# Small pads between the operand buffers of a float32r feed-forward stage

## The chip, the cores and the metric

The kernel runs on one core of one Trainium2 chip. The metric is the device time of one execution in microseconds (us), as the median over runs.

## The reference

One layer with 2048 rows of 640 channels. A modulation row (`c`, `w_mod`) gives scales and shifts. A state-space convolution over the rows comes first, then a gated feed-forward network (FFN) with an inner width of 1728:

```python
h = _layernorm(x, axis=-1) * (1 + ca) + sa
x = x + ga * _A_ref(h, A_log_A_real, A_A_imag, A_C_real, A_C_imag, A_log_dt, A_D_skip)
h = _layernorm(x, axis=-1) * (1 + cb) + sb
x = x + gb * _B_ref(h, B_w1, B_w3, B_w2)
...
    def _B_ref(x, w1, w3, w2):
        gate = jnp.einsum("bsd,df->bsf", x, w1)
        up = jnp.einsum("bsd,df->bsf", x, w3)
        h = _silu(gate) * up
        out = jnp.einsum("bsf,fd->bsd", h, w2)
        return out
```

`_A_ref` builds a convolution kernel for each channel and applies it with FFTs. All arrays are float32.

## The kernel before

**Stages.** About the first 390 us belong to the convolution: tables and kernels for five blocks of 128 channels, and Fourier products as matmuls in plain float32. Then come some tens of microseconds in which the first pieces of the FFN are made ready (`tail_tasks`, with `gates` at line 1302), and from about 440 us to the end the FFN (`ffn`, line 1412). The order of the work up to the FFN is a planner's (`Plan.place`, by ranks and durations); in the FFN it is the order of the code.

**The FFN's products.** Each float32 operand is split into a high and a low part in the type float32r (`split`: ScalarE rounds, VectorE takes the difference), and a product is three matmuls: high weights by high rows, high weights by low rows, low weights by high rows (`three`, line 852). Every one has a 128x128 weight tile and streams 512 columns of a "moving" operand. The 2048 rows are four blocks of 512, taken two at a time. `groups` (line 1422) goes over the tiles of 128 inner channels; for two blocks at once it saves one product in eight by sums and differences of operands (`factors`, `x_sums`), so that a tile takes 54 matmuls into gate and up values (`X`, `c` in the profile) and 15 into the output sums (`acc`, `down`, line 1032). `late` (line 1454) then does the second block's output sums and transposes.

**Buffers.** A tile is asked of a pool by its tag; tags get addresses in the order in which they are first asked for. Each address below is in bytes within a partition. Two pools matter here.
- `wp`, on the left side of the memory: the split weights `wh0`, `wl0` ... `wh7`, `wl7` (1024 bytes each, made by `pair`, line 816), the raw weights `wr`, the split output weights `w2` (three buffers) and their raw form `w2r`. All of these sizes are multiples of 512, and the pool begins at 35744, so every weight tile that a matmul reads begins at residue 416 modulo 512.
- `fp`, on the right side: among others the moving operands `x0h`, `x0l` ... `x8h`, `x8l` (`x_new`, line 739) and `ah`, `al` (lines 883 and 1342). These sizes are multiples of 512 too, and every moving operand begins at residue 480 modulo 512 (`x0h` at 136160, `ah` at 183264 and 185312).

The pool `const` already holds a tile named `pad` of 128 bytes that nothing reads or writes (line 311): `cols` before it ends at 1788, rounded to 1792, and `sc` after it begins at 1920.

Of the kernel before, what the change touches and what calls it, by code (L numbers as in the profile page):

```python
# [10 lines left out]
F32 = mybir.dt.float32  # L11
F32R = mybir.dt.float32r
# [6 lines left out]
P = 128  # L19
# [9 lines left out]

EXPS = ((0, 0, 0, 64.0), (0, 1, 0, 1.0), (1, 0, 0, 512.0), (1, 1, 4, 8.0), (1, 2, 0, 8.0))  # L30
LOADS = 20
G0 = 17
SIGN = -2 ** 31
RANKS = """
# [113 lines left out]
class InOrder:  # L148

    def __init__(self, k, eng):  # L150
        self.k, self.eng, self.prev = k, eng, None
# [130 lines left out]
class K:  # L282
    def __init__(self, tc, ctx, io):
        self.tc, self.nc, self.ctx = tc, tc.nc, ctx
        for k, v in io.items():
            setattr(self, k, v)

# [449 lines left out]
        return (t[:, k % 2 if n == 2 else 0] for t in X[g])  # L737

    def x_new(self, tag, name, n):
        return [self.fp.tile([P, n, 512], F32R, name=f"{tag}{x}{name}", tag=tag + x) for x in "hl"]  # L740

    TS = (("T1", "x2"), ("T2", "x3"), ("T3", "x4"), ("T4", "x6"))

# [70 lines left out]
        return t[:, 0], t[:, 1]  # L814

    def pair(self, i, name):
        return tuple(self.wp.tile([P, 2, P], F32R, name=f"w{x}{i}_{name}", tag=f"w{x}{i}") for x in "hl")

    def operand(self, i, name, v, eng):

# [62 lines left out]
    def hidden_split(self, b, m, a, eng):  # L883

        A = self.nc.scalar
        ah, al = (self.fp.tile([P, 512], F32R, name=f"a{x}{b}_{m}", tag=f"a{x}", bufs=2) for x in "hl")
        if m < 13:
            self.split(ah, al, a, eng)
            return ah, al
        th = self.tmp(f"t{b}_{m}")  # L890
        A.activation(ah[:64], a[64:], AF.Copy)
        A.activation(th[64:], ah[:64].bitcast(F32), AF.Copy)
        self.nc.vector.tensor_sub(ah[64:], a[64:], th[64:])
        return ah, None
# [169 lines left out]
    def paced(self, dst, src):  # L1064

        ins = self.nc.sync.dma_start(dst, src)
        n = len(self.pace)
        if 1 < n < LOADS:
            self.tc.add_manual_dep(ins.ins, self.pace[-2 if n < 6 else -4].ins.name,
# [3 lines left out]
    def tail_tasks(self, border, cut):  # L1073
# [10 lines left out]
        def add(name, eng, took, f, after=(), rank=0.0, **kw):  # L1084
            plan.add(name, eng, took, f, after, rank, own=True, **kw)
# [3 lines left out]
        def load(name, src, dst, size, after=(), pool="change", **kw):  # L1089
            i = n_load[0]  # L1090
            n_load[0] += 1
            loads.append(name)
            early = i < LOADS
            add(name, "SP", 0, lambda: self.paced(dst(), src), [pool, *after] + (loads[max(i - 2, 0):i][:1] if early else ["izb0"]), -60 + .1 * i,
# [180 lines left out]
        def plain(b, tiles, p, rank, after):  # L1275
# [23 lines left out]
            for r, m in enumerate(tiles):  # L1299
                gates(b, m, banks, f"{b}.{m}", last, names, (rank if b or m == 1 else G0) + .5 + .1 * r)  # L1300

        def gates(b, m, banks, n, last, names, r):
            t = {}

            def alloc(x):
                return self.h_tile(m) if b else self.tmp(f"a{b}{m}")

            def th():
                t[0] = self.tmp(f"th{n}")
                if m < 13:  # L1310
                    return A.activation(t[0], banks[m][0], AF.Tanh, scale=0.5)
                t[1] = alloc(m)
                A.activation(t[0][64:], banks[m][0][:64], AF.Tanh, scale=0.5)
                A.activation(t[1][64:], banks[m][0][:64], AF.Copy)

            def st():
                if m < 13:
                    t[1] = alloc(m)
                    V.scalar_tensor_tensor(t[1], t[0], 1.0, banks[m][0], op0=ALU.add, op1=ALU.mult)
                else:  # L1320
                    V.scalar_tensor_tensor(t[1][64:], t[0][64:], 1.0, t[1][64:], op0=ALU.add, op1=ALU.mult)

            def mu():
                if m < 13:
                    V.tensor_mul(t[1], t[1], banks[m][1])
                else:
                    V.tensor_mul(t[1][64:], t[1][64:], banks[m][0][64:])
                if b:
                    self.h[m] = t[1]
            one = [("tmp", 1)]  # L1330
            two = [("tmp", 1, "*")] if b == 0 else []
            room = ["T1l.0", "T1l.1", "T2l.0"] if b and m == 1 else []
            add("gt" + n, "ACT", .6 if m < 13 else 1.2, th, last + (room if m == 13 else []), r, take=one + (two if m == 13 else []))
            add("gs" + n, "DVE", .69, st, ["gt" + n] + (room if m < 13 else []), r, take=two if m < 13 else [],
                give=[("tmp", "gt" + n)] + (names[m, 0] if m < 13 else []))
            add("gm" + n, "DVE", .69, mu, ["gs" + n], r, give=names[m, n_of(m) - 1])
            if b:
                return
            key = [("tmp", ("gs" if m < 13 else "gt") + n + "*")]
            if m < 13:  # L1340
                def hi():
                    t[4], t[5] = (self.fp.tile([P, 512], F32R, name=f"a{x}0_{m}", tag=f"a{x}", bufs=2) for x in "hl")
                    self.high(t[4], t[1])
                add("gh" + n, "ACT", .6, hi, ["gm" + n] + (["dn0.0"] if m == 1 else []), r + .2)
                add("gl" + n, "DVE", .69, lambda: self.low(t[4], t[5], t[1]), ["gh" + n], r + .2, give=key)
            else:
                add("gl" + n, "DVE", 1.9, lambda: t.__setitem__(6, self.hidden_split(0, 13, t[1], V)), ["gm" + n], r + .3, take=[("tmp", 1)], give=key)
                add("gx" + n, None, 0, None, ["gl" + n], give=[("tmp", "gl" + n)])

            def down():  # L1350
                if m == 0:
                    self.acc = self.accumulators(0)
                self.down(self.acc, m, (t[4], t[5]) if m < 13 else t[6], (w2[m][:, 0], w2[m][:, 1]), m == 0, False)
            add("dn" + n, "PE", 3.42 if m < 13 else 2.28, down, ["gl" + n, f"w2l{m}"] + {0: [f"v1.{k}" for k in range(KT)] + ["pp1.4"], 13: ["dn0.0", "pq0.4"], 1: ["dn0.13"]}[m], r + 1, give=[("w2", f"w2h{m}")])
# [13 lines left out]
        f = {}  # L1368
# [807 lines left out]
```

## Time and profile before

| what | value |
|---|---|
| median of 3 runs | 973.41 us (972.67 to 974.1) |
| the profiled execution's own time | 972.31 us |
| span of the profiled execution | 970.5 us |
| mean granted TensorE clock | 0.975 |
| TensorE matmuls busy | 859.9 us, 89% |
| weight loads busy | 681.8 us, 70% |
| VectorE busy | 702.0 us, 72% |
| ScalarE busy | 546.4 us, 56% |
| GpSimd busy | 340.5 us, 35% |
| DMA | 127.31 MB, mean 131 GB/s |

PE stands for TensorE's matmuls, PEld for its weight loads, DVE for VectorE, ACT for ScalarE, POOL for GpSimd. The duration of a matmul in the profile holds a fixed latency besides the time in which its columns stream, so matmuls overlap; the step from one start to the next is what a row of them costs.

### The profile page before, as it was taken

Reading aid. Unit: us, or ns where it says so; the run is one execution under the profiler, and the core shown is the slowest. Engines: PE = TensorE matmul, PEld = TensorE weight load, DVE = VectorE, ACT = ScalarE, POOL = GpSimd, SP = SyncE. Lnnn points to the kernel's source line nnn. Section 1 sums busy time; section 2 is a strip of 40 time slices with the busy share of each in tenths; the row PEclk is TensorE's granted clock in tenths of the full one; section 3 lists DMA queues with packets and bytes.
Section 4 is the critical chain, followed back from the end, with each engine's and each line's share of the span. In section 5 each row is a group of like instructions: output and inputs, shape, how many; then the busy total and the mean of one; then the engine's idle time right before and its main releaser. Section 6 shows DMA issues by size and latency. Waiting matters only on the chain.

```text
span 970.5 us, 20551 instructions
## 1 busy us (share of the span) xinstructions
PE 859.9 (89%) x7985; PEld 681.8 (70%) x7985; DVE 702.0 (72%) x1395; ACT 546.4 (56%) x1022; POOL 340.5 (35%) x371
## 2 busy tenths in 40 slices
PE   1464787889899997899999999999999999999997
PEld 1132665767778884677777778888788888888775
DVE  7998899999999968886767677557456464645422
ACT  6877788979888851564434455346444344443412
POOL 1797889879799600002111111000011212120000
PEclk9996999999999999799999999999999999999999
DMA  9955453723425268935434422276342322220374
GB/s 218 275 168 191 111 136 95 177 66 106 111 80 152 74 159 206 241 118 182 122 120 139 122 96 68 82 209 194 112 134 64 102 77 86 82 82 28 108 220 133
DMA packets 110506, 127.31 MB, mean 131 GB/s; under 512 B 10568, under 2 KB 90696, under 8 KB 109128
## 3 DMA queue, kind: packets, MB, share of 16 engines
q1 hardware_dynamic: 109032, 125.21, 45.3%
q8 instruction: 63, 1.03, 0.5%
q10 hardware_dynamic: 1376, 0.79, 0.3%
q14 instruction: 35, 0.29, 0.1%
HBM read 95.82 MB, written 30.15 MB: 130 GB/s over the span
## 4 chain that ended last, share of the span: by engine, by line
PE 70%; DVE 17%; ACT 5%; issue 4%; DMA 3%; POOL 1%; SPq 1%; ACTq 0%; DVEq 0%
PE c L157 19%; PE acc L157 18%; PE X L157 12%; PE ps L157 4%; PE gu L157 3%; DVE yy L157 3%; PE kps L157 3%; PE fz L157 2%; PE fk L157 2%; DVE fp L157 2%; PE fh L157 2%; DVE hn L157 2%; DVE xx L157 2%; DVE xb L157 1%; ACT tr L157 1%
## 5 line engine op out<-in xcount | busy, mean ns | idle before, releaser
L157 PE MATMUL acc<-ah,w 128*128 128x512 f32 x560 | 173.2, 395 | 2.4 <-DMA w<-w2d 1.7
L157 PEld LDWEIGHTS acc<-ah,w 128*128 128x128 f32 x560 | 103.7, 188 | 26.4 <-issue 2.1
L157 PE MATMUL acc<-al,w 128*128 128x512 f32 x260 | 102.4, 394 | 0.0
L665 DVE TENSOR_TENSOR wl<-s,wh 128x256 fp32r<-128x256 f32 x92 | 38.9, 423 | 67.5 <-ACT wh L664 67.1
L841 POOL TENSOR_TENSOR s<-wr 128x256 f32<-128x256 f32 x22 | 16.4, 744 | 187.8 <-DMA wr<-in_w 94.8
L157 POOL TENSOR_TENSOR ph<-p,p 128x1024 int32<-128x1024 int32 x40 | 79.2, 1979 | 8.2 <-ACT tr L157 8.0
L664 ACT ACTIVATE wh<-s 128x256 fp32r<-128x256 f32 x92 | 37.6, 410 | 78.5 <-PE X L157 58.1
L157 PE MATMUL kps<-yy,xx 128*32 128x64 f32 x2560 | 51.8, 234 | 28.6 <-DVE xx L157 21.4
L157 DVE TENSOR_TENSOR yy<-yy,tr 128x512 f32<-128x512 f32 (+1 forms) x80 | 75.3, 943 | 1.2 <-ACT tr L157 0.6
L157 PEld LDWEIGHTS kps<-yy,xx 128*32 128x32 f32 x2560 | 45.1, 116 | 38.3 <-issue 22.0
L664 ACT ACTIVATE wh<-wr 128x256 fp32r<-128x256 f32 x92 | 38.4, 418 | 56.0 <-PE X L157 42.3
L842 POOL TENSOR_TENSOR s<-s,wr 128x256 f32<-128x256 f32 x22 | 16.6, 755 | 134.0 <-issue 133.9
L902 ACT ACTIVATE t<-g 128x512 f32<-128x512 f32 x44 | 27.8, 632 | 52.7 <-DVE g L866 52.7
L157 ACT ACTIVATE tr<-ph,hpi 128x512 f32<-128x512 f32 x80 | 54.6, 690 | 4.4 <-DVE xx L157 2.7
L157 PEld LDWEIGHTS acc<-al,w 128*128 128x128 f32 x260 | 48.9, 188 | 10.8 <-DVE al L665 0.3
L871 DVE SCALAR_TENSOR_TENSOR g<-t,g 128x512 f32<-128x512 f32 x48 | 33.7, 702 | 31.3 <-ACT t L902 29.3
L157 POOL TENSOR_TENSOR yy<-e,e 128x512 f32<-128x512 f32 x48 | 52.4, 1109 | 8.8 <-PE kps L157 5.9
L157 DVE TENSOR_TENSOR xx<-tr,xx 128x512 f32<-128x512 f32 x80 | 54.3, 680 | 1.1 <-ACT tr L157 1.1
L157 PE MATMUL ps<-wk,ks 128*64 128x128 f32 x640 | 42.4, 285 | 13.6 <-DVE ks L157 8.9
L157 ACT ACTIVATE tr<-ph 128x512 f32<-128x512 int32 x80 | 47.3, 598 | 12.4 <-DVE yy L157 6.5
L157 PE MATMUL ps<-wk,xb 128*64 128x128 f32 x640 | 46.1, 295 | 6.3 <-ACT sp L157 3.0
L157 PEld LDWEIGHTS ps<-wk,ks 128*64 128x64 f32 x640 | 37.0, 143 | 20.3 <-ACT hn L157 6.6
(448 smaller groups left out, 2379.7 us busy)
## 6 DMA issues: line engine op xcount, KB each, us to landing
w<-w2d SPq DMA_DIRECT2D x42, 640.0 KB, 3.9
wr<-in_w SPq DMA_DIRECT2D x50, 320.0 KB, 3.9
zd<-zt SPq DMA_DIRECT2D x40, 256.0 KB, 2.9
w2d<-w SPq DMA_DIRECT2D x14, 640.0 KB, 3.5
xs<-in_x SPq DMA_DIRECT2D x16, 320.0 KB, 11.3
hs<-hb SPq DMA_DIRECT2D x20, 256.0 KB, 2.5
xb<-hs SPq DMA_DIRECT2D x20, 256.0 KB, 4.9
iz<-zd SPq DMA_DIRECT2D x32, 160.0 KB, 5.0
```

Of the source, the lines that this page charges most:

```text
L157: self.prev = self.k.order(f(*a, **kw), self.prev)
L664: self.nc.scalar.activation(H, v, AF.Copy)
L665: eng.tensor_tensor(Lo, v, H.bitcast(F32), op=ALU.subtract)
L841: eng.tensor_tensor(s[0], u[:, 0:2], u[:, 2:4], op=ALU.add)
L842: eng.tensor_tensor(s[1], s[0], g[:, 0:2], op=ALU.subtract)
L871: V.scalar_tensor_tensor(g, th, 1.0, g, op0=ALU.add, op1=ALU.mult)
L902: tanh = lambda o, i: A.activation(o, i, AF.Tanh, scale=0.5)
```

## The change

A dictionary `PAD` gives, by tag, a number of units of 32 bytes. When one of these tags is first asked for, a small tile that nothing uses is taken from the same pool just ahead of it (`apart`), and all later buffers of the pool move up. In `fp` the entry `end` brings the sum to 512 bytes, so that what lies ahead of the first pad and behind the last keeps its residue.

```diff
+PAD = {'wh1': 1, 'wl1': 1, 'wh4': 1, 'wh3': 1, 'wl3': 1, 'wh7': 2, 'wh2': 2, 'wl2': 2, 'wl5': 1, 'wh6': 1, 'wl6': 2, 'x0l': 1, 'x4h': 2, 'x5h': 2, 'x2h': 2, 'x3h': 2, 'end': 7}
...
+        self.placed = set()
...
     def x_new(self, tag, name, n):
-        return [self.fp.tile([P, n, 512], F32R, name=f"{tag}{x}{name}", tag=tag + x) for x in "hl"]
+        return [self.fp.tile([P, n, 512], F32R, name=f"{tag}{x}{name}", tag=self.apart(self.fp, tag + x)) for x in "hl"] + ([] if tag != "x6" or self.apart(self.fp, "end") else [])
...
     def pair(self, i, name):
-        return tuple(self.wp.tile([P, 2, P], F32R, name=f"w{x}{i}_{name}", tag=f"w{x}{i}") for x in "hl")
+        return tuple(self.wp.tile([P, 2, P], F32R, name=f"w{x}{i}_{name}", tag=self.apart(self.wp, f"w{x}{i}")) for x in "hl")
+
+    def apart(self, pool, tag):
+        if tag not in self.placed:
+            self.placed.add(tag)
+            if PAD.get(tag):
+                pool.tile([P, 8 * PAD[tag]], F32, name="pad" + tag)
+        return tag
```

The two places that make `ah` and `al` ask through `apart` as well; `PAD` has no entry for them. No instruction is added, removed or moved.

With the buffers in the order in which they lie before, adding up the pads gives these residues modulo 512:

| moving operand | before | after | | weights | before | after |
|---|---|---|---|---|---|---|
| x0h | 480 | 480 | | wh0, wl0 | 416 | 416, 416 |
| x0l, x1h, x1l, x7h, x7l | 480 | 0 | | wh1, wl1 | 416 | 448, 480 |
| x4h, x4l, ah, al | 480 | 64 | | wh4, wl4, wh3, wl3 | 416 | 0, 0, 32, 64 |
| x5h, x5l, x8h, x8l | 480 | 128 | | wh7, wl7, wh2, wl2 | 416 | 128, 128, 192, 256 |
| x2h, x2l | 480 | 192 | | wh5, wl5, wh6, wl6 | 416 | 256, 288, 320, 384 |
| x3h, x3l, x6h, x6l | 480 | 256 | | w2 | 416 | 384 |

More of the change, by code (lines that the diff above doesn't have):

```diff
@@ L885, in hidden_split @@
         A = self.nc.scalar
-        ah, al = (self.fp.tile([P, 512], F32R, name=f"a{x}{b}_{m}", tag=f"a{x}", bufs=2) for x in "hl")
+        ah, al = (self.fp.tile([P, 512], F32R, name=f"a{x}{b}_{m}", tag=self.apart(self.fp, f"a{x}"), bufs=2) for x in "hl")
         if m < 13:
@@ L1341, in hi @@
                 def hi():
-                    t[4], t[5] = (self.fp.tile([P, 512], F32R, name=f"a{x}0_{m}", tag=f"a{x}", bufs=2) for x in "hl")
+                    t[4], t[5] = (self.fp.tile([P, 512], F32R, name=f"a{x}0_{m}", tag=self.apart(self.fp, f"a{x}"), bufs=2) for x in "hl")
                     self.high(t[4], t[1])
```

## The prediction, made before the changed kernel was seen

> **What bounds the kernel now.** I read the page's busy shares and the chain that ended last first: where does a change to the FFN's buffers meet the path?
>
> ```profile
> PE 859.9 (89%) x7985; PEld 681.8 (70%) x7985; DVE 702.0 (72%) x1395; ACT 546.4 (56%) x1022; POOL 340.5 (35%) x371
> ...
> PE 70%; DVE 17%; ACT 5%; issue 4%; DMA 3%; POOL 1%; SPq 1%; ACTq 0%; DVEq 0%
> PE c L157 19%; PE acc L157 18%; PE X L157 12%; PE ps L157 4%; PE gu L157 3%; DVE yy L157 3%; PE kps L157 3%; PE fz L157 2%; PE fk L157 2%; DVE fp L157 2%; PE fh L157 2%; DVE hn L157 2%; DVE xx L157 2%; DVE xb L157 1%; ACT tr L157 1%
> ```
>
> Of the chain, `c`, `acc`, `X` and `gu` are 52% of the span, and they are the FFN's float32r matmuls, the ones whose two operands the pads move. Next the busy time by stretches, for one tile of inner channels and for ten, and the waits of PE from 400 us on:
>
> ```profile
> 726.32:884.25 157.93, 157.93 (x691) 129.58 (x691) 88.82 (x170) 68.15 (x151) 28.89 (x39) 1.00 0.27 80
> ...
> 742.11:757.90 15.79, 15.79 (x70) 12.96 (x70) 8.89 (x17) 6.81 (x16) 2.95 (x4) 1.00 0.28 83
> ```
> ```profile
> PE gu L157 <- DVE a L157: 2.0, 3, 1.3
> PE acc L157 <- DMA w<-w2d: 1.7, 1, 1.7
> ```
>
> The columns are the stretch, its length, and the busy time of PE, PEld, DVE, ACT and POOL, then the granted clock. PE is busy throughout at clock 1.00; DVE has 8.89 of 15.79 us, ACT 6.81. The longest two waits of PE in 570 us come to 3.7 us. So a nanosecond more or less on each of these matmuls reaches the end of the kernel. A tile has 69 of them (54 and 15; the 70th and the 691st are the ones cut by the edge), and 157.93 us over 690 is 228.9 ns from start to start.
>
> How many are there? The groups of instructions, first and last of each kind:
>
> ```profile
> L157 PE MATMUL acc<-ah,w 128*128 128x512 f32 x560 | 173.2, 395 | 2.4 <-DMA w<-w2d 1.7 <-ACT oc L1044 0.7
> L157 PE MATMUL acc<-al,w 128*128 128x512 f32 x260 | 102.4, 394 | 0.0
> L157 PE MATMUL c<-x5h,wh 128*128 128x512 f32 x48 | 19.8, 412 | 0.1
> ...
> L157 PE MATMUL X<-x0h,wl 128*128 128x512 f32 x48 | 18.9, 393 | 0.0
> ...
> L157 PE MATMUL X<-x0h,wh 128*128 128x512 f32 x48 | 18.8, 392 | 0.4 <-DVE late L1053 0.4
> ...
> L157 PE MATMUL X<-x8h,wh 128*128 128x512 f32 x24 | 9.3, 389 | 0.0
> ...
> L157 PE MATMUL gu<-x0h,wl_u 128*128 128x512 f32 x10 | 4.1, 413 | 0.0
> ...
> L157 PE MATMUL gh<-x0h,wl_u 128*128 128x512 f32 x2 | 0.8, 394 | 0.0
> ```
>
> 820 for `acc`, 24 groups of 48 and 6 of 24 for `X` and `c` (1296), 150 for `gu` and 30 for `gh` (by the loops of both functions named `plain`, their rows in groups of 10, 5 and 2): 2296 matmuls. At 228.9 ns they are 525.6 us of the profiled execution's 972.31. The 120 that stream `x0h` (48 + 48 + 10 + 10 + 2 + 2) keep its residue; 2176 stream an operand that moves.
>
> **Is there something to gain in one matmul?** The plain float32 matmuls give the price of a column. One tile's view for the transposes `to` and for the inverse `iy`, and the timeline of four transposes in a row:
>
> ```profile
> L157 PE MATMUL to<-ident,oc x80: 270/272/330, 638.8 to 965.0; 128*128 128x128 f32 x80
> ...
> L157 PE MATMUL iy<-iz,late x24: 590/592/643, 369.0 to 379.0; 128*64 128x512 f32 x24
> L157 PE MATMUL iy<-xb,late x8: 592/592/592, 379.4 to 380.7; 128*64 128x512 f32 x8
> ...
> 912.74 0.60 PE L157 MATMUL to<-ident,oc 128*128 128x128 f32 x4
> ```
>
> 384 columns more take 592 - 272 = 320 ns, so a column takes 0.833 ns and 165 ns are fixed latency. Four transposes take 0.60 us, so their step is (600 - 272) / 3 = 109 ns, 2.6 above 128 columns. If a float32r column takes half of a float32 one (an estimate: its step, 228.9 / 512 = 0.447 ns, is near that), 512 columns take 213.3 ns and the step would be 215.9. The FFN pays 13.0 ns more, 29.8 us over 2296 matmuls. Where do they come from? Two readings of the trace narrow it. First, a matmul beside which no weights load:
>
> ```profile
> 931.68 0.19 PEld L157 LDWEIGHTS acc<-al,w 128*128 128x128 f32 x1
> 933.99 0.30 PEld L157 LDWEIGHTS acc<-ah,w 128*128 128x128 f32 x2 [2.12 <-issue]
> ...
> 931.90 0.40 PE L157 MATMUL acc<-al,w 128*128 128x512 f32 x1
> 934.02 0.71 PE L157 MATMUL acc<-ah,w 128*128 128x512 f32 x2 [1.72 <-DMA w<-w2d]
> ```
>
> The one at 931.90 has no load beside it until 933.99, and it takes 0.40 us, no less than its neighbours with loads. So the 13 ns are not lost to the weight load, and the relation of weights to moving operand, which the pads make various, costs nothing as it is now. In a sentence that the sum does not need: the Trainium skill ("TensorE: Matmul & The Clock Gate", step-by-step part) says that PE has two independent read ports and that loading the next weights takes no read bandwidth from the running matmul; this row agrees with it.
>
> Second, the same buffers in two late stretches:
>
> ```profile
> L157 PE MATMUL acc<-ah,w x33: 387/392/482, 913.1 to 925.9; 128*128 128x512 f32 x33
> L157 PE MATMUL acc<-al,w x16: 388/392/397, 913.6 to 925.7; 128*128 128x512 f32 x16
> ...
> L157 PE MATMUL acc<-ah,w x58: 397/397/398, 934.8 to 954.6; 128*128 128x512 f32 x58
> L157 PE MATMUL acc<-al,w x29: 397/397/398, 935.3 to 954.9; 128*128 128x512 f32 x29
> ...
> 936.66 0.40 PE L157 MATMUL acc<-al,w 128*128 128x512 f32 x1
> ...
> 940.86 0.40 PE L157 MATMUL acc<-al,w 128*128 128x512 f32 x1
> ```
>
> In the second every matmul takes 397 ns, and from 936.66 to 940.86 lie 18 steps of 233.3 ns, 4.4 more than elsewhere. The addresses are the same and so is the clock: the cost above the columns is not fixed, it depends on how the stream lies in time. This swing of 4.4 ns is the only one that the trace shows.
>
> **The change part by part.** *Weights at 16 residues.* By the first reading: nothing to gain. What other relations cost is not in the trace, where all 2296 have one (480 - 416 = 64). *Moving operands.* All begin at 480, which is 32 past a multiple of 64; afterwards the 2176 begin at multiples of 64. A stream of 2048 bytes from 480 touches 33 blocks of 64 bytes, and 32 when it begins on one. If the source is read in such blocks, each saves 16 columns of 0.417 ns, 6.7 ns, 14.5 us in all. With blocks of 128 bytes the 1032 that come to lie at 0, 128 or 256 (those of `x0l`, `x1`, `x7`, `x5`, `x8`, `x3`, `x6`) save 13.3 ns each, 13.8 us. With blocks of 32 nothing changes. Bounds for one matmul are thus the whole 13.0 ns as gain and, towards slower, the 4.4 ns of the second stretch. Between them I take a gain of 4.4 ns, the one size by which the trace shows this step to vary, with the sign from the alignment, which gets better for every operand that moves: 2176 x 4.4 = 9.6 us. The DVE and ACT slack of a tile (6.9 and 9.0 us) is not used up by the 0.3 us that a tile then loses. *The rest.* `w2` moves from 416 to 384; its loads land beside matmuls but for the one wait of 1.7 us above, which stays. The FFN's buffers shift by up to 512 bytes over those of the stage before, which all end ahead of it: nothing, and at most the longest wait there, 1.3 us, either way.
>
> **Sum.** 972.31 - 9.6 = 962.7 for the profiled execution; that lies 1.1 us under the median of the runs, so for the median 973.41 - 9.6 = 963.8 us.
>
> **The rivals.** *Slower: the streams settle in the worse step.* The 228.9 is a rhythm that the present single relation of all operands keeps from matmul to matmul; with relations that change at each product it may be lost, and every matmul takes 397 ns as in the second stretch. Place: all 2296; price 4.4 ns, 10.1 us, so 983.5 us; it decides as soon as more matmuls settle there than gain. For it: 87 matmuls in a row did settle there, without any change of address, and the lone matmul took 0.40 too, so 397 may be the natural state and the quicker one the exception. Against it: after most of the FFN's gaps the quick rhythm came back. A relation could also cost more than 4.4 ns; no row bounds that. *No change: 973.4 us.* The 13 ns may be float32r's own, whatever the address. For it: the `iy` rows above, where `iz` lies at 416 and `xb` at 480, take 592 both; yet they stream at half the rate. In this rival the pads change addresses and nothing else. The Trainium skill ("SBUF — State Buffer", specifications) gives lines of 16 bytes; by that page multiples of 32 cut no line anew and the time would stay 973.4; no run here shows the size of a line. That the pads have no effect on addresses at all is unlikely: the unused `pad` of 128 bytes holds its place between `cols` and `sc`.
> *Much faster:* all 13.0 ns go from 2176 matmuls, 28.3 us, 945.1 us. By the page on TensorE (the Trainium skill, "TensorE: Matmul & The Clock Gate", back-to-back issue gap) 512 columns step by about 216 ns, an estimate close to the 215.9 above; the trace has 228.9, so that page does not describe float32r as it stands here.
>
> **How the numbers follow.** About 0.2% (2 us) is what a measurement can tell from no change here. Faster, 0.43: of it a quarter for half the excess or more. Slower by the worse step, 0.39, a third of it beyond 4.4 ns. No change, 0.18. The likeliest is faster, 963.8 us, with its own range of 945.1 to 971.4. Both signs hold much, so the whole range goes from 945.1 (the floor of the sum) to 985.0 (the worse step and the 1.3 us of the other waits, rounded up); only dearer relations lie beyond.
>
> **What would show it.** If alignment is the cause, the groups that stream `x0h` stay at 392 to 393 ns and the others fall; a tile in `groups` goes from 15.79 to 15.49 us. If the worse step wins, medians are 397 and a tile takes 16.10. If a relation to the weights costs, groups of one moving operand differ by `wh` and `wl`. I am wrong if the medians do not move, or if those of `acc`, whose relation goes from 64 to 192, rise.

## The result: 979.4 us, slower, and the profile after

The changed kernel takes 979.41 us (median of 3 runs, 979.18 to 981.98) where the kernel before takes 973.41. The ratio on record is 1.0068, 95% interval 1.0049 to 1.0088 (the two medians by themselves give 1.0062). The forecast was 963.8 us; the time lies inside its range, on the other side of no change. The profiled execution took 981.98 us with a span of 980.2. Times and ratios here and below are of executions in the chip's faster state; one of e3 (1004.65 us) and one of e6 (1253.04 us) were in the slower one and are left out.

The page of the changed kernel, busy shares and chain:

```profile
PE 870.2 (89%) x7985; PEld 685.4 (70%) x7985; DVE 701.8 (72%) x1395; ACT 546.5 (56%) x1022; POOL 340.6 (35%) x371
...
PE c L158 19%; PE acc L158 17%; PE X L158 12%; PE ps L158 5%; PE gu L158 3%; DVE yy L158 3%; DMA xs<-in_x 3%; PE fz L158 3%; PE kps L158 3%; PE fk L158 2%; DVE fp L158 2%; PE fh L158 2%; DVE xx L158 2%; DVE hn L158 2%; ACT tr L158 1%
```

The same instructions, and DVE, ACT and POOL busy as before to 0.2 us; PE is busy 10.3 us longer and its weight loads 3.6. The waits of PE from 400 us on, and the same ten tiles and one tile by stretches (columns as in the prediction):

```profile
PE gu L158 <- DVE a L158: 2.0, 3, 1.3
PE acc L158 <- DMA w<-w2d: 1.4, 1, 1.4
```
```profile
733.56:893.63 160.07, 160.07 (x691) 129.63 (x691) 88.99 (x170) 68.30 (x151) 28.76 (x39) 1.00 0.26 79
749.57:765.58 16.01, 16.01 (x70) 12.96 (x70) 8.90 (x17) 6.83 (x16) 2.94 (x4) 1.00 0.28 83
```

The waits are as before and the granted clock is 1.00 again, but ten tiles take 160.07 us instead of 157.93: 232.0 ns from matmul to matmul instead of 228.9. The time is in the step itself. Which matmuls? The groups of instructions:

```profile
L158 PE MATMUL acc<-ah,w 128*128 128x512 f32 x560 | 175.2, 398 | 1.9 <-DMA w<-w2d 1.4 <-ACT oc L1053 0.6
L158 PE MATMUL acc<-al,w 128*128 128x512 f32 x260 | 102.9, 396 | 0.0
...
L158 PE MATMUL X<-x0h,wh 128*128 128x512 f32 x48 | 19.2, 399 | 0.4 <-DVE late L1062 0.4
...
L158 PE MATMUL X<-x4hT,wl 128*128 128x512 f32 x48 | 19.0, 397 | 0.0
...
L158 PE MATMUL X<-x4hT,wh 128*128 128x512 f32 x48 | 18.7, 390 | 0.0
L158 PE MATMUL X<-x0h,wl 128*128 128x512 f32 x48 | 18.6, 389 | 0.0
```

Two things are to be seen. `x0h` has not moved, yet one of its groups rose from 392 to 399 and the other fell from 393 to 389. And groups that stream one and the same buffer now differ by 7 to 10 ns with the weights, `wh` or `wl`. Before, the two groups of `x0h` were 1 ns apart and those of `x4hT` 4:

```profile
L157 PE MATMUL X<-x4hT,wl 128*128 128x512 f32 x48 | 18.9, 393 | 0.0
...
L157 PE MATMUL X<-x4hT,wh 128*128 128x512 f32 x48 | 18.7, 389 | 0.0
```

This points to where the moving operand lies against the weights, and not to where it lies by itself; the experiments below test it.

The chain that ended last gives the step by the kind of output, for one tile and for the last run of `acc`; first the kernel before, then the changed one (start, length, both in us):

```profile
873.95 2.06 PE X L157 x9
876.01 3.43 PE c L157 x15
879.44 3.43 PE acc L157 x15
...
934.02 24.36 PE acc L157 x102
```
```profile
865.06 2.10 PE c L158 x9
867.16 2.08 PE X L158 x9
869.25 3.48 PE c L158 x15
872.73 3.49 PE acc L158 x15
...
943.62 24.36 PE acc L158 x102
```

Fifteen matmuls of `acc` cost 60 ns more, 4 ns each; the fifteen of `c` 50 more, 3 ns each; the nine of `X` 20 more, 2 ns each. The last 102 take 24.36 us in both: there the kernel before already ran at 233.3 ns. By the ten tiles, 3.1 ns on 2296 matmuls are 7.1 us. In the profiled executions the stretch from the 159th of these matmuls to the end of the span (440.02 to 970.5 before, 443.89 to 980.2 after) grew by 5.8 us, which is nearly all of the 6.0 us between the medians. The other 3.9 us between the two spans lie ahead of it, where the clock was granted lower in this one execution (0.85 and 0.90 against 0.90 and 0.95 in the first two stretches of 100 us); before, then after:

```profile
0.00:100.00 100.00, 41.52 (x633) 23.90 (x633) 87.83 (x171) 75.12 (x143) 66.43 (x80) 0.90 0.74 210
100.00:200.00 100.00, 80.00 (x1554) 67.69 (x1556) 96.39 (x186) 83.36 (x141) 86.48 (x90) 0.95 0.52 128
```
```profile
0.00:100.00 100.00, 40.65 (x633) 22.73 (x633) 86.40 (x171) 74.11 (x142) 66.12 (x79) 0.85 0.75 210
100.00:200.00 100.00, 81.22 (x1520) 68.84 (x1520) 95.09 (x183) 82.46 (x141) 85.18 (x89) 0.90 0.51 128
```

### The profile page after: what moved, and what is told of

Same layout as the page of the kernel before. It is cut to its first block, busy times and chain, and to the rows that moved or that the text cites. A ratio compares the mean times of both kernels' runs of the same rounds, so it can differ in the third digit from the quotient of the medians.

```text
span 980.2 us, 20551 instructions
## 1 busy us (share of the span) xinstructions
PE 870.2 (89%) x7985; PEld 685.4 (70%) x7985; DVE 701.8 (72%) x1395; ACT 546.5 (56%) x1022; POOL 340.6 (35%) x371
## 4 chain that ended last, share of the span: by engine, by line
PE 70%; DVE 14%; ACT 5%; DMA 4%; issue 3%; POOL 1%; SPq 1%; ACTq 0%; DVEq 0%; POOLq 0%
PE c L158 19%; PE acc L158 17%; PE X L158 12%; PE ps L158 5%; PE gu L158 3%; DVE yy L158 3%; DMA xs<-in_x 3%; PE fz L158 3%; PE kps L158 3%; PE fk L158 2%; DVE fp L158 2%; PE fh L158 2%; DVE xx L158 2%; DVE hn L158 2%; ACT tr L158 1%
## 5 line engine op out<-in xcount | busy, mean ns | idle before, releaser
L158 PE MATMUL acc<-ah,w 128*128 128x512 f32 x560 | 175.2, 398 | 1.9 <-DMA w<-w2d 1.4
L158 PEld LDWEIGHTS ps<-wk,xb 128*64 128x64 f32 x640 | 44.5, 221 | 9.8 <-ACT sp L158 3.4
```

The source lines that it names most:

```text
L158: self.prev = self.k.order(f(*a, **kw), self.prev)
```

## The experiments

Three theories stood at first. R: the relation, moving address minus weight address, sets the step. O: the own residue of the moving operand sets it. V: that residues vary from product to product is what costs. "Relation" below is modulo 256. Steps of single matmuls are differences of consecutive starts in the trace; a settled step is the mean after the first third of a row.

**e1_map: every relation by itself.** The layer is replaced by rows of 48 float32r matmuls, 128x128 by 512 columns, for moving operands at 480, 0 and 64 and sixteen relations each; then rows after a pause, alternately at 64 and 192.

```python
for m in (480, 0, 64):
    for d in range(0, 512, 32):
        block(f"m{m}d{d}", m, (m - d) % 512, ps, COUNT)   # moving at m, weights at m - d
```

> It leaves out the whole layer and runs only float32r matmuls of 512 columns: 48 in a row for each of 48 blocks (m480d64 is the block whose moving operand begins at residue 480 modulo 512 and whose weights lie 64 bytes behind it), then 12 blocks of 24 after a pause. Theory R, the relation (moving minus weights, modulo 512) sets the step: the 16 relations give different steps, equal for the three residues 480, 0 and 64; 229 ns at 64 and 233 at 192, as the changed kernel's output sums showed (233.4). Theory O, the moving operand's own residue sets it: all 16 relations alike, 229 at 480 and 233 at 64. Theory V, only a change of residue from one matmul to the next costs: all 48 blocks at 229. Theory S, the state in which a row starts: the blocks after a pause differ among themselves at one relation (229 or 233.3).

The chain by own residue (sixteen rows each), and two rows after a pause, at 64 and at 192:

```profile
27.35 178.25 PE m480d L37 x768
205.60 178.24 PE m0d L37 x768
383.84 178.28 PE m64d L37 x768
...
574.24 5.78 PE gap1d L37 x24
580.39 5.88 PE gap1d L37 x24
```

The own residue changes 768 matmuls by 0.04 us: O falls. The settled step by relation, the same for 256 more:

| relation | 0 | 32 | 64 | 96 | 128 | 160 | 192 | 224 |
|---|---|---|---|---|---|---|---|---|
| ns | 226.7 | 233.4 | 228.9 | 233.3 | 233.3 | 234.3 | 233.3 | 233.3 |

The kernel before had the second best of the eight, and `acc` was moved to one of the bad ones. In each of six pairs after a pause the row at 64 came back to 229 and the row at 192 to 233, so the pause didn't decide (theory S falls; V had all 48 rows at 229 and falls here too).

**e2_rel192: one uniform relation in the layer.** All weights move together, the moving operands stay: 192 everywhere, no variety.

```diff
-PAD = {'wh1': 1, 'wl1': 1, ... 'end': 7}
+PAD = {'wh0': 12}
```

> Before, with one pad of 384 bytes ahead of all weights: all residues stay uniform, moving 480, weights 288, relation 192 instead of 64. Theory R: every step as the changed kernel's output sums, 233.4 ns, so +4.2 ns on 2296 matmuls, +9.6 us, 983 us. Theory O and theory V: as before, 973.4 us.

980.77 us, ratio 1.0074 (1.0053 to 1.0096). Ten tiles:

```profile
731.59:892.59 161.00, 161.00 (x691) 129.72 (x691) 89.01 (x170) 68.37 (x151) 29.09 (x39) 1.00 0.26 78
```

161.00 / 690 is 233.3 ns, the step of the map. As slow as the change, with no variety and no moving operand touched: R holds, V isn't needed for it. R had 983 us; the time is 2 us less than that, though the step is the one expected.

**e3_moving_only and e4_weights_only: half of the change each.**

```diff
+PAD = {'x0l': 1, 'x4h': 2, 'x5h': 2, 'x2h': 2, 'x3h': 2, 'end': 7}       # e3
+PAD = {'wh1': 1, 'wl1': 1, ... 'wl5': 1, 'wh6': 1, 'wl6': 2}             # e4
```

> Only the pads of the moving operands (weights stay at 416; relation of the output sums 160). Theory O: as the whole change, 979.4 us. Theory R: another set of relations (64 to 96, 160, 224, 288, 352), so another time than the whole change; the size is open until the map. Theory V: slower than before, between 973.4 and 979.4 us.

> Only the pads of the weights (moving operands all at 480; relation of the output sums 96). Theory O: as before, 973.4 us. Theory R: another time than before, the size open until the map; theory V: slower than before, between 973.4 and 979.4 us.

982.93 us, ratio 1.0095 (1.0067 to 1.0123), and 980.85 us, ratio 1.0066 (1.004 to 1.0091). V and O had at most 979.4. Neither half is clearly cheaper than the whole: each alone already takes `acc` off 64 (to 160 and to 96) and most of the other products with it. R had left the size open; the table at the end of this section gives it from the map.

**e5_fine: steps of 4 bytes.** Rows of 32 at relations 0, 4 ... 252, and rows whose matmuls alternate, so that the pair's own relation and the one to the next weights differ.

```python
for d in range(0, 256, 4):
    block(f"r{d}b", (256, 256), (256 - d, 256 - d), 32)
for own, nxt in ((64, 192), (192, 64), (0, 128), (128, 0), (64, 64)):
    ...
    block(f"own{own}next{nxt}b", m, w, 48)
```

> It leaves out the layer and runs only float32r matmuls of 512 columns: 32 in a row at each relation (moving minus weights) from 0 to 252 bytes in steps of 4 (r64b is 64), then five blocks of 48 in which moving operand and weights alternate between two residues. Theory R with lines of 32 bytes or more: the steps within a group of 32 bytes are equal, 226.7, 233.3, 228.9, 233.3, 233.3, 234.3, 233.3, 233.3 ns. Theory R with finer lines: values between, perhaps under 226.7. In the alternating blocks, if a matmul's relation to its own weights counts, own64next192b takes 228.9 and own192next64b 233.3, own0next128b 226.7 and own128next0b 233.3; if its relation to the weights that load beside it (the next matmul's) counts, the other way round.

```profile
26.47 7.25 PE r0b L36 x32
33.73 7.26 PE r4b L36 x32
40.99 7.46 PE r8b L36 x32
...
152.47 7.46 PE r68b L36 x32
...
197.18 7.59 PE r92b L36 x32
204.77 7.47 PE r96b L36 x32
212.24 7.26 PE r100b L36 x32
```

The step depends on single words of 4 bytes: 8 bytes beside relation 0 a row costs 0.2 us more, and from 96 to 100 it falls by 0.2. Settled steps go from 226.7 (0, 4, 100, 124, 136) to 238.2 (92), and 233.3 is the commonest; none is below 226.7. The alternating rows took 230.0 (own 64, next 192), 230.0 (192, 64), 228.3 (0, 128), 230.0 (128, 0) and 228.9 (64, 64): neither of the two relations sets the step alone, and neither set of expected values came true.

**e6_rel0 and e9_rel0_again: the best relation for all.** Weights 64 bytes up, moving operands where they were.

```diff
+PAD = {'wh0': 2}
```

> Before, with one pad of 64 bytes ahead of all weights: residues uniform, moving 480, weights 480, relation 0. Theory R with the map: 226.7 instead of 228.9 ns on 2296 matmuls, 5.1 us faster than before, 968 us. Rival, the relation matters only as far as it was 64 (a tuned optimum): slower, 980 us as at 192.

> All weights moved by 64 bytes, moving operands as before: every relation 0 modulo 256. Theory R (the relation of moving operand and weights sets the step): 2.2 ns less on each of 2296 matmuls, 5.0 us, 968 to 971 us and a ratio of 0.995 to 0.997; step 226.7 ns, and the groups of X and c no longer differ by wh and wl. Theory V (only that the residues are various costs): 973.

First 970.49 us beside 973.6, ratio 0.9961 (0.994 to 0.9982); its profiled execution is the one of 1253.04 us, at a mean clock of 0.662, and its rows aren't compared. Then, in e9, 969.22 us beside 972.88, ratio 0.9962 (0.9944 to 0.998); R had 968 and then 968 to 971 us. Ten tiles of e9, and a tile of the chain:

```profile
726.90:883.30 156.40, 156.40 (x691) 129.55 (x691) 88.54 (x170) 67.93 (x151) 28.70 (x39) 1.00 0.26 80
```
```profile
826.17 2.04 PE X L158 x9
828.21 3.40 PE c L158 x15
831.61 3.40 PE acc L158 x15
```

156.40 / 690 is 226.7 ns, as in the map. One pad of 64 bytes makes a version that is 0.4% faster than the kernel before.

**e7_both96: pads, but the old relation.** Weights and moving operands both move by 96 bytes; the operands lie at 64 and 0, the relation stays 64.

```diff
+PAD = {'wh0': 3, 'x0h': 3, 'end': 13}
```

> Before, with 96 bytes ahead of all weights and 96 ahead of all moving operands: moving 64, weights 0, relation 64 kept. Theory R: as before, 973.2 us. Theory O (own residue, or the mere presence of pads): as the whole change, 6 us slower.

972.45 us, ratio 0.9986 (0.9967 to 1.0005), and ten tiles take 157.93 us, to the digit what they took before:

```profile
727.17:885.10 157.93, 157.93 (x691) 129.62 (x691) 88.71 (x170) 68.05 (x151) 28.77 (x39) 1.00 0.26 79
```

Two stretches differ from the kernel before, and the relation can't be the cause, since it is 64 in both. The last run of `acc` took 24.36 us there and takes 23.96 here; an early run of 15 takes 3.50 us here and 3.43 there. First this kernel, then the one before:

```profile
424.90 3.50 PE acc L158 x15
...
934.38 23.96 PE acc L158 x102
```
```profile
424.62 3.43 PE acc L157 x15
```

In the slow stretches, from 418 to 453 us here and the last one of the kernel before, the single steps are 233, 233, 234, over and over; elsewhere they are near 226, 229, 232. So a row at relation 64 can run in two rhythms, as the prediction's second reading had it, and what chooses between them is not known.

**e8_width: is it the weight load or the stream?** Narrower weights, shorter streams, and bfloat16 as a control.

```python
for d in (0, 64, 192):
    for cols in (128, 64, 32):
        block(f"w{cols}r{d}b", d, cols, 512, 48)
...
        block(f"n{width}r{d}b", d, 128, width, 48)        # width 384, 256
    block(f"bf16r{d}b", d, 128, 512, 48, H, G, 2)
```

> Leaves out the layer: only rows of matmuls, 48 each, at relations (moving minus weights) 0, 64 and 192, with 128, 64 or 32 weight columns (w blocks), with 384 or 256 moving columns (n blocks), and in bfloat16. Theory W (the excess is lost to the weight load that runs beside the stream): with 512 moving columns the excess over a floor near 215.9 ns (17 ns at relation 192, 13 at 64, 11 at 0) shrinks with the weight columns, to about a half with 64 (224, 222, 221) and a quarter with 32 (220, 219, 219), and with 128 weight columns it is about the same number of ns for 384 and 256 moving columns. Theory S (it belongs to the moving stream alone, by column): the step stays at 233, 229 and 227 with 64 and 32 weight columns and goes with the moving columns, 175 and 117 at relation 192. Bfloat16: if the relation acts through float32r's way of reading only, about 216 at all three relations; if through the port whatever the type, the same order as in float32r.

| settled step, ns | relation 0 | 64 | 192 |
|---|---|---|---|
| 128 weight columns, 512 moving | 226.7 | 228.9 | 233.3 |
| 64, 512 | 230.0 | 228.3 | 232.8 |
| 32, 512 | 231.7 | 231.0 | 231.7 |
| 128, 384 | 173.3 | 173.3 | 174.7 |
| 128, 256 | 120.0 | 117.8 | 117.8 |
| bfloat16, 128, 512 | 215.8 | 215.8 | 215.8 |

Neither theory stands as written. Against W: with 32 weight columns the excess doesn't shrink to a quarter. Against S: the width of the weights does change the step, by 5.0 ns upwards at relation 0 and 1.6 downwards at 192, and the order of the relations depends on the length of the stream (at 256 columns, 0 is the worst). At relation 0 the excess over (columns x 0.4167 + 2.5 ns, which gives bfloat16's 215.8) is the same 10.8 ns for 512, 384 and 256 columns; at 64 it grows with the columns. Bfloat16 takes the same at all three relations. So here the effect is float32r's, and it needs both operands; as bfloat16 also reads half the bytes, the type and the bytes aren't told apart, and how the two reads meet was not found.

**e10_spread0: various residues, nearly every pair at 0.** Eighteen pads and `end` (the change has sixteen and `end`), chosen so that 2188 of the 2296 products have relation 0; `w2` asks through `apart` too.

```diff
+PAD = {'wh0': 2, 'wh1': 1, 'wh4': 2, 'wh3': 2, 'wh7': 5, 'wh2': 3, 'wh5': 7, 'wh6': 7, 'w2': 1, 'x1h': 1, 'x7h': 1, 'x4h': 1, 'ah': 1, 'x5h': 1, 'x8h': 5, 'x2h': 1, 'x3h': 1, 'x6h': 1, 'end': 3}
```

> Operands at many residues as in the change, but the pads chosen so that 2188 of the 2296 products have moving operand and weights at relation 0 modulo 256 (the rest at others), and 1935 also to the next product's weights. Theory R: 969 to 972 us, nearly as with one relation 0 for all. Theory V (variety of residues costs as such, as the slower rival of the prediction had it): 979 to 983 us.

974.52 us, ratio 1.002 (1.0002 to 1.0038): between the two, and 5.3 us over e9 in the same comparison. The relation of the pair alone doesn't give this time. Ten tiles, and the timeline where `acc` takes over from `c` in one tile (start and length of the bar, in us; between two lines stand the two matmuls of `ah`):

```profile
727.78:886.32 158.54, 158.54 (x691) 129.51 (x691) 88.97 (x170) 68.11 (x151) 28.76 (x39) 1.00 0.26 79
```
```profile
607.24 0.39 PE L158 MATMUL acc<-al,w 128*128 128x512 f32 x1
...
607.94 0.40 PE L158 MATMUL acc<-al,w 128*128 128x512 f32 x1
...
608.63 0.39 PE L158 MATMUL acc<-al,w 128*128 128x512 f32 x1
...
609.31 0.39 PE L158 MATMUL acc<-al,w 128*128 128x512 f32 x1
...
609.99 0.39 PE L158 MATMUL acc<-al,w 128*128 128x512 f32 x1
```

Three matmuls take 0.70, 0.69, 0.68 and 0.68 us: the row starts at 233 ns a step and comes down to 227. The single steps of such a row, nearly the same in every tile:

```
230, 224, 231, 236, 228, 233, 230, then 227, 227, 226, 227, 227, 226 ...
```

Here the stream needs about seven matmuls until it keeps the step of its relation. `acc` has 15 matmuls of one residue in a tile and gets there: 87 of its 150 steps in ten tiles lie between 226 and 228 ns. The runs of `X` and `c` have six or three matmuls between two changes, and 157 of their 540 steps lie there. Ten tiles take 2.14 us more than in e9; with 12 changes of residue in a tile that is about 18 ns for each. Two theories of such a change are told apart next. T: it upsets the stream for some matmuls. P: each product costs what its own pair and the load beside it cost, without memory.

**e11_switch: the changes by themselves.** Rows of 96, always at relation 0; after each k matmuls both operands move together by s bytes, or back.

```python
z = s // 4 if (i // k) % 2 else 0
a, b = 512 * (i % 2) + z, 128 * (i % 4) + z
nc.tensor.matmul(t, W[:, b:b + 128], M[:, a:a + 512], start=i == 0, stop=i == n - 1)
```

> Leaves out the layer: rows of 96 matmuls, every one at relation 0 to its own weights; after each k matmuls (k = 32, 16, 8, 4, 2, 1) both operands move together by s bytes (s = 64, 128, 192) or back, the last row never. Theory T (each change of residue upsets the stream, which then needs about seven matmuls to come back to its quick step, as the run with spread residues shows: 230, 224, 231, 236, 228, 233, 230, then 227): a change costs 15 to 25 ns, so the mean step is 227 to 227.5 at k = 32, 228 at 16, 229 to 230 at 8, and from 4 down the row never settles, 229 to 233; after each change five to seven unsettled steps are seen. Theory P (each product costs what its own pair and the load beside it cost, no memory): only the one step at a change is longer, by at most the 6.7 ns of the worst common relation: 226.9 at k = 32, 227.1 at 16, 227.5 at 8, 228.4 at 4, 230 at 2, 233 at 1.

| mean step after the first third, ns | k = 32 | 16 | 8 | 4 | 2 | 1 |
|---|---|---|---|---|---|---|
| s = 64 | 227.5 | 228.3 | 231.3 | 228.3 | 232.3 | 231.7 |
| s = 128 | 227.0 | 227.3 | 227.9 | 229.2 | 231.7 | 228.3 |
| s = 192 | 227.5 | 228.3 | 231.3 | 228.3 | 232.4 | 231.7 |

For 64 and 192 bytes T holds in kind, and its sizes were too small: after a change in one direction ten steps are off (228, 229, 234, 235, 225, 230, 236, 229, 232, 231), in the other three (229, 233, 231); at k = 16 the mean is 1.7 ns up, 27 ns for each change, where T had 15 to 25, and at k = 8 it is 231.3, where T had 229 to 230. For 128 bytes only two steps are off (233, 231), about 10 ns, which is nearer to P; but P had 233 for k = 1, and no row has that. At k = 4, T had 229 or more for all and two of three rows have 228.3, so the size isn't to be had from a simple count.

**e12_acc64: undo the part with the longest rows.** The change, with `w2` another 128 bytes up: `acc` back at 64.

```diff
-PAD = {..., 'wl6': 2, 'x0l': 1, ...}
+PAD = {..., 'wl6': 2, 'w2': 4, 'x0l': 1, ...}
...
-        return self.wp.tile([P, 2, D], F32R, name=name, tag="w2", bufs=3)
+        return self.wp.tile([P, 2, D], F32R, name=name, tag=self.apart(self.wp, "w2"), bufs=3)
```

> The change with w2 moved by another 128 bytes: the 820 matmuls of acc get back their relation 64, the pads of all other operands stay. Theory R (the pair's relation sets the step of a long row, 233.3 against 229.6 for acc): 3.0 us less than the change, 975.5 to 977 beside a time of 973 before, ratio 1.003 to 1.005, acc medians near 393 to 395. Theory V (that residues are various costs, in all rows alike): as the change, ratio 1.006 to 1.008.

977.22 us, ratio 1.0038 (1.0024 to 1.0053), where R had 975.5 to 977 and 1.003 to 1.005. In the chain only `acc` moves, from 3.49 to 3.44, while the pieces of `c` and `X` stay as in the change:

```profile
862.14 2.10 PE c L158 x9
864.24 2.08 PE X L158 x9
866.32 3.48 PE c L158 x15
869.80 3.44 PE acc L158 x15
```

Ten tiles take 159.40 us, 0.67 less than in the change. So the relation of `acc` is about 2 of the change's 6 us (the intervals of the two ratios overlap a little), and the rest belongs to `X` and `c`.

All layers side by side. "By the map" is an estimate: the sum of e1's steps over the 69 pairs of a tile, each at its relation, times ten. "For 2296" is (ten tiles of this kernel - 157.93) / 690 x 2296.

| kernel | ten tiles, us | by the map, us | for 2296, us | ratio, interval |
|---|---|---|---|---|
| e9, all at 0 | 156.40 | 156.42 | -5.1 | 0.9962 (0.9944 to 0.998) |
| e7, all at 64 | 157.93 | 157.94 | 0.0 | 0.9986 (0.9967 to 1.0005) |
| e10, spread, pairs at 0 | 158.54 | 156.42 | +2.0 | 1.002 (1.0002 to 1.0038) |
| e12, change, acc at 64 | 159.40 | 159.04 | +4.9 | 1.0038 (1.0024 to 1.0053) |
| the change | 160.07 | 159.70 | +7.1 | 1.0068 (1.0049 to 1.0088) |
| e4, weights only | 160.67 | 160.65 | +9.1 | 1.0066 (1.004 to 1.0091) |
| e2, all at 192 | 161.00 | 160.98 | +10.2 | 1.0074 (1.0053 to 1.0096) |
| e3, moving only | 161.10 | 161.02 | +10.5 | 1.0095 (1.0067 to 1.0123) |

The relations alone thus give five of the eight kernels to 0.1 us, and of the 2.14 us that the change adds they give 1.77: in a tile of the change 29 pairs lie at 192, 14 at 0, 8 at 64 and 18 at other relations. The 0.37 left over fit the changes of residue, as in e10, but are not shown to be that: e3 and e4 also change residue within a tile and have hardly anything left over (0.08 and 0.02 us).

The step in ten tiles orders the times, but for e4 and the change, whose intervals overlap. The column for 2296 is on the high side for the slow kernels; one piece of that is the last run of `acc`, which stood at 233 ns before, too.

## Why the prediction was wrong

**What bounds the kernel: right.** The longer step reached the end: 7.1 us by the ten tiles, 5.8 in the FFN's stretch; neither of PE's two longest waits grew, and slack on DVE and ACT took nothing back.

**The price of a column and the floor: half right.** The floor of 215.9 ns, worked out from the transposes, is bfloat16's step to 0.1 ns (e8). For float32r none of the 64 relations of e5 reached it: the lowest step is 226.7. So the "much faster" rival at 945.1 us wasn't to be had by these addresses; of the 13.0 ns of excess 2.2 go, by one 64-byte pad.

**The first reading: the step that failed.** From one matmul of 0.40 us with no weight load beside it, the prediction concluded that the relation of weights to moving operand costs nothing, and the sum put it at nothing. By the map the relations of the change cost 2.55 ns a matmul, an estimate of 5.9 us over 2296, beside 6.0 measured; the relation was the cause (e1, e2, e7, e9). A recorded duration is not a step: it holds the fixed latency, its end is modelled, and the neighbours at 0.40 ran in the slow stretch of 233 ns, so that the comparison was with the wrong neighbours too. The matmul at the same place of the changed kernel, where the relation is 192, shows how little the row says; it takes the same 0.40 us (0.39 in e9, at 0):

```profile
941.85 0.40 PE L158 MATMUL acc<-al,w 128*128 128x512 f32 x1
```

The Trainium skill ("TensorE: Matmul & The Clock Gate", step-by-step part) gives PE two independent read ports, so that the load would take nothing from the running matmul; the prediction said that this row agreed. Measured, moving the weights alone by 64 bytes takes 2.2 ns off each step (e9) and by 384 puts 4.4 on (e2): for float32r the step isn't independent of where the weights lie, and the measurement decides. The about 216 ns for 512 columns that the Trainium skill gives by its formula for the gap of a single matmul ("TensorE: Matmul & The Clock Gate", back-to-back issue gap) agree with bfloat16's 215.8.

**The sign: wrong.** It came from the alignment of the moving operand to 64 bytes, a gain of 9.6 us that no row had shown. Own residues of 480, 0 and 64 gave the same 178.2 us (e1), and `x0h`, which kept its residue, changed by +7 and -4 ns.

**The size: in part luck.** The 4.4 ns of the second stretch happens to be also the spacing between the step at relation 64, 228.9, and the commonest step, 233.3; the second stretch itself lay at 64. The slower rival took it for all 2296 matmuls, 983.5 us; the mean was 3.1 ns, since 22 of a tile's 69 pairs lie at relations 0 and 64. The rival's reason, a rhythm that changing relations break, isn't what slows the long rows, as a uniform 192 costs no less (e2). But the rival wasn't empty: rows are slow for some matmuls after a change of residue (e11), and a kernel with nearly every pair at its best relation took 974.5 us instead of 969.2 with such changes in it (e10). That 979.4 us lies in the stated range is owed to the range, which held both signs, and not to the mechanism forecast.

**No change, by lines of 16 bytes** (the Trainium skill, "SBUF — State Buffer", specifications): multiples of 32 do change the time, and 4 bytes can be enough for it (e5, from 96 to 100).

**What would show it** named the two signs that came true: groups of one moving operand that differ by `wh` and `wl`, and a rise of `acc`, whose relation went from 64 to 192. The prediction thus had the right test in hand; it was ruled out by one row read for more than it says. What stays open: why the relation acts modulo 256, and why some stretches at relation 64 run at 233 ns (the last 102 matmuls of the kernel before, 418 to 453 us of e7) and others at 229, as six rows after pauses in e1 did.

## What to carry to other kernels

In a PE-bound row of float32r matmuls, the addresses of both operands belong to the tuning. For 128x128 weights and streams of 512 columns, put moving operand and weights at the same residue modulo 256 and keep one residue for all buffers (for other shapes make the map first: at 256 columns relation 0 was the slowest of the three in e8). Then check the step from start to start over some hundred matmuls, not the duration of one. A trace in which an address takes only one value says nothing on what other values cost; a small map of the relations by itself, which costs one run, gives the sign of this change and five sixths of its size in ten tiles. When pads are spread for variety, count what each product's pair becomes, and how many matmuls lie between two changes of it.

## What was not expected of the hardware

- The settled step of 128x128 by 512 float32r matmuls goes from 226.7 to 238.2 ns with (moving - weights) modulo 256 (e5); bfloat16 has 215.8 at all three relations tried (e8).
- The step has a memory: after a change of residue by 64 bytes three to ten matmuls are off, by 128 bytes two (e11). And one relation, 64, has two rhythms: steps near 226, 229, 232 ns, or 233, 233, 234 (the kernel before and e7).
- Narrower weights need not make the stream quicker: when they shrink from 128 to 32 columns the step rises from 226.7 to 231.7 ns at relation 0 and falls from 233.3 to 231.7 at 192 (e8).
